# Linear attention with a cosine router: transposes and state updates set at other places in TensorE's and VectorE's order

## The chip, the cores and the metric

The kernel runs on one core of a Trainium2 chip. A core has five engines, each of which works through its own list of instructions in order: TensorE (PE: matmuls and transposes), VectorE (DVE), ScalarE (ACT), GpSimd (POOL) and SyncE (SP, which issues most of the transfers). They wait for each other through semaphores. The metric is the time of one execution on the device, in microseconds (us); several runs are taken and their median is given.

## The reference

Two blocks, one behind the other. The first is a linear attention with a decaying state, for 4 batches, 8 heads, 768 steps and 48 columns a head; the second sends every row of its output to one of 8 experts by a cosine similarity.

```python
for t in range(S):                                    # S = 768, per batch and head
    cur = np.einsum('bhd,bhe->bhde', u[None] * kt, vt)
    y[:, :, t] = np.einsum('bhd,bhde->bhe', rt, state + cur)
    state = w[None, :, :, None] * state + np.einsum('bhd,bhe->bhde', kt, vt)
x = y.transpose(0, 2, 1, 3).reshape(3072, 384)
...
logits = xn @ en.T / tau                              # normed rows, 8 experts
expert_idx = np.argmax(logits, axis=1)
out[mask] = gate_w[mask, None] * (np.maximum(x[mask] @ w1[e], 0) @ w2[e])
```

All numbers are float32.

## The kernel before

**Attention in turns.** The 768 steps are cut into 6 chunks of 128, and a chunk again into two halves of 64. A turn `t` does one chunk of two of the four batches, so there are 12 turns (`TURNS`); `c, bp = divmod(t, 2)` are its chunk and its pair of batches, and `u` (0 or 1) is the batch within the pair. The heads are worked on in 4 pairs.

What a turn does on each engine:

- GpSimd scales the loaded R and K by powers of the decay (`scale_r`, `scale_k`, L377 and L373), half a turn to a turn ahead.
- TensorE transposes R and K of each batch, four 128x128 blocks each (`turn_in`, L393, into banks D0 and D1 for the first batch, D2 and D3 for the second). ScalarE copies them to SBUF (`take_in`: R at L409, K at L407), and VectorE makes a second R, times u (`own_r`, L420).
- TensorE computes the scores (`scores`, L433, 32 small matmuls a batch, into the same D banks). VectorE masks them and puts in the diagonal's own terms (`mask` L448, `own_terms` L455).
- TensorE adds up outer products of K and V (`outer`, L469, 64 small matmuls, into bank U0 for the chunk's first half and U1 for the second). VectorE adds U0 to the state (`half_state`, L485), then U1 to that (`next_state`, L490), and GpSimd applies the decay (`decay_state`, L496).
- In the next turn's time, TensorE makes the outputs: masked scores times V (`with_v`, L524, in two phases of 32), with the state times R between them (`with_state`, L543: 32 matmuls with the state at the chunk's start, `s` = 0, which chunk 0 has not, and 32 with the half state, `s` = 1). `between` (ScalarE, L512) reads one column of each output bank, so that the second phase starts after the first has drained.
- ScalarE copies the outputs to SBUF (`take_y`, L550), TensorE transposes them to rows (`turn_y`, L558, four blocks a batch, into U0 for the first batch and U1 for the second: the banks of the outer products), ScalarE copies the rows (`take_x`, L562), SyncE writes them to DRAM (`keep_x`, L587), and ScalarE takes the sum of squares (`squares`, L593).
- Once in two turns the router's work of a chunk is put in between: `logits` (L600), `turn_logits` (L622), `ranks` (L684 to L687), `put` (L867), and small steps on VectorE; `choose_a` (GpSimd, L639 and L640) works on the sums of squares.

The small matmuls use the array in tiles: 48 or 64 rows by 48 or 64 columns, four at a time. The transposes and `put` use all of it (128 by 128), `logits` strips of 32 columns.

**What sets the order.** Nothing is reordered by a scheduler. `attention` gives each step a time in a plan (`plan.at(time, function, ...)`); the plan is sorted by time and written out, and each engine runs what it has in that order. The times are no clock: they only say what comes before what. A turn is `PERIOD` = 9.4 units long; `at` is its start, `before` and `nxt` the starts of the turns on either side, and `end` that of the last one. So TensorE's order in the middle turns is: scores of both batches, `turn_logits` or `ranks`, `with_v` phase 0, `with_state` (both), `put`, `turn_in` of R and K of the first batch of the next turn, `with_v` phase 1, `outer` of both batches, `turn_in` of R and K of the second batch, `turn_y` of both batches, `logits`. VectorE's order in the second half of a turn is `half_state`, `next_state`, `own_r` of the second batch.

Loads of R, K and V are issued by SyncE some three turns ahead, each once TensorE has reached the instruction that was the last written out before it (`k.last`).

**The experts.** After attention the rows are gathered by expert with indirect transfers, and each expert's two layers follow (L1165 for the first two, then L1243 and L1364/L1383, where products of sums take the place of some matmuls). This part takes the time from some 131 us on.

Of the kernel before, what the change touches and what calls it, by code (L numbers as in the profile page):

```python
# [70 lines left out]
def halves(s):  # L71
    return slice(s * HC, (s + 1) * HC)
# [272 lines left out]
def of(ring, t):  # L345
    return ring[t % len(ring)]
# [111 lines left out]
    )  # L458


def outer(k, t):
    Kw, V = of(k.Kw, t), of(k.V, t)
    last = t // 2 == NCH - 1
    for u in range(2):
        for p in range(NP):
            for s in range(1 if last else 2):
                for par in range(2):
                    h, col = 2 * p + par, (u * NP + p) * D
                    k.last = k.nc.tensor.matmul(  # L469
                        k.U[s][par * DP : (par + 1) * DP, col : col + D],  # L470
                        Kw[halves(s), u, h, :], V[halves(s), u, h, 0:D],
                        start=True, stop=True, skip_group_check=True,
                    )
# [407 lines left out]
def attention(k):  # L881

    plan = Plan()
    P = PERIOD
    end = (TURNS - 1) * P
    for t in range(TURNS):
        at = t * P
        c, bp = divmod(t, 2)
        before, nxt = at - P, at + P
        for i in range(6 if t else 0):  # L890
            when = at - 3 * P + 0.5 + 1.55 * i
            if t < 4:

                if t < 3 and i > 3:
                    continue
                plan.at(when, load, k, t, i // 2 if t > 2 else i % 2, i % 2 if t > 2 else i // 2, slice(0, H), False)
                if t < 3 and i == 3:
                    for v in ((0,), (1, 2))[t - 1]:
                        for w in range(2):
                            plan.at(when + 0.1 * v + 0.01, load, k, v, 2, w, slice(0, H), False)  # L900
                continue
            for j in range(2):
                plan.at(when + 0.75 * j, load, k, t, i // 2, i % 2, slice(j * NP, (j + 1) * NP))
        for u in range(2):
            for which in range(2):

                place = which if t else 1 - which
                if t:
                    plan.at(before + 1.0 + 2 * u + place, scale_k if which else scale_r, k, t, u)
                plan.at(before + 3.3 + 2.35 * u + 0.47 * place, turn_in, k, t, u, which)  # L910
                plan.at(before + 3.8 + 2.4 * u + 0.6 * place, take_in, k, t, u, which)
            plan.at(before + (4.0 if t else 4.75) + 2.6 * u, own_r, k, t, u)
            plan.at(at + 0.9 * u, scores, k, t, u)
            for par in range(2):
                plan.at(at + 0.9 + 1.5 * u + 0.36 * par, mask, k, t, u, par)
                plan.at(at + 1.65 + 1.5 * u + 0.4 * par, own_terms, k, t, u, par)
        if t < TURNS - 1:
            plan.at(at + 4.75, outer, k, t)
            plan.at(at + 5.6, half_state, k, t)
        else:  # L920
            plan.at(at + 5.0, outer, k, t)
            plan.at(at + 5.3, half_state, k, t)
        if c < NCH - 1:
            plan.at(at + 6.2, next_state, k, t)
            plan.at(at + 6.8, decay_state, k, t)
        if t < TURNS - 2:
            a = (1.8, 2.3, 3.3, 4.25, 5.0, 6.65, 7.4, 8.4)
            plan.at(nxt + a[0], with_v, k, t, 0)
            plan.at(nxt + a[1], with_state, k, t)
            plan.at(nxt + a[2], between, k, t)  # L930
            plan.at(nxt + a[3], with_v, k, t, 1)
            for par in range(2):
                plan.at(nxt + a[4] + 0.6 * par, take_y, k, t, par)
            for u in range(2):
                plan.at(nxt + a[5] + 0.45 * u, turn_y, k, t, u)
                plan.at(nxt + a[6] + 0.5 * u, take_x, k, t, u)
                plan.at(nxt + a[6] + 0.1 + 0.5 * u, keep_x, k, t, u)
                plan.at(nxt + a[7] + 0.7 * u, squares, k, t, u)
        else:

            for when, fn, *args in (
                (
                    (3.0, with_v, 0), (3.5, with_state), (4.6, between), (5.6, with_v, 1),
                    (5.65, take_y, 0), (5.7, take_y, 1), (7.6, turn_y, 0), (7.75, take_x, 0), (7.9, turn_y, 1),
                    (7.76, keep_x, 0), (8.5, take_x, 1), (8.51, keep_x, 1), (9.5, squares, 0), (9.55, squares, 1),
                ),
                (
                    (6.8, with_v, 0), (6.82, with_state, (0,)), (7.5, with_state, (1,)), (7.7, between),
                    (7.8, with_v, 1), (8.2, take_y, 0), (8.4, take_y, 1), (10.0, turn_y, 0), (10.02, turn_y, 1),
                    (10.4, take_x, 0), (10.41, keep_x, 0), (10.5, take_x, 1), (10.51, keep_x, 1),  # L950
                    (10.7, squares, 0), (10.75, squares, 1),
                ),
            )[t - TURNS + 2]:
                plan.at(end + when, fn, k, t, *args)
        if bp == 1 and c < NCH - 1:
            plan.at(nxt + 7.6, logits, k, c)
            plan.at(nxt + 8.6, take_logits, k, c)
            then = nxt + P
            plan.at(then + 1.78, turn_logits, k, c)
            if c < NCH - 2:  # L960
                plan.at(then + 2.42, keep_logits, k, c)
                plan.at(then + 6.9, choose_a, k, c)
                plan.at(then + 7.5, choose, k, c)
                plan.at(then + 8.9, scale, k, c)
                plan.at(then + 9.0, exps, k, c)
                then += P
                plan.at(then + 1.79, ranks, k, c)
                plan.at(then + 2.42, placed, k, c)
                plan.at(then + 7.5, places, k, c)
                plan.at(then + 8.7, gate, k, c)  # L970
                plan.at(then + 8.8, values, k, c)
                plan.at(then + 8.9, rows_of, k, c)
                plan.at(then + P + 3.25, put, k, c)
                plan.at(then + P + 3.95, collect, k, c)
            if c == SETTLE[0]:
                plan.at(then + 2.43, count, k, c)
                plan.at(then + 5.0, settle, k, c)
                plan.at(then + 5.05, settled, k)

    c = NCH - 2  # L980
    for t, fn, *args in (
        (1.0, choose_a, k, c),
        (3.96, first_lists, k, 0),
        (4.0, keep_logits, k, c),
        (4.2, choose, k, c),
        (5.5, scale, k, c),
        (6.3, exps, k, c),
        (6.85, ranks, k, c),
        (6.9, placed, k, c),
        (6.95, count, k, c),  # L990
        (7.3, places, k, c),
        (7.4, settle, k, c),
        (7.45, sort_embeddings, k),
        (7.5, sort_counts, k),
        (8.4, gate, k, c),
        (8.8, values, k, c),
        (8.9, rows_of, k, c),
        (11.2, put, k, c),
        (11.25, collect, k, c),
        (11.3, first_lists, k, 1),  # L1000
        (11.35, settled, k),
    ):
        plan.at(end + t, fn, *args)
# [3 lines left out]
    c = NCH - 1  # L1007
# [790 lines left out]
def kernel(  # L1798
# [43 lines left out]
    with tc.manual_schedule(), ExitStack() as long_ctx:  # L1842
        n.long = long_ctx.enter_context(tc.tile_pool(name="long", bufs=1))
        with ExitStack() as attention_ctx:
            n.aconst = attention_ctx.enter_context(tc.tile_pool(name="aconst", bufs=1))
            rings(n)
            build_first(n)
            n.rt = attention_ctx.enter_context(tc.tile_pool(name="rt", bufs=2))
            attention(n)
        with ExitStack() as experts_ctx:  # L1850
            n.gp1 = experts_ctx.enter_context(tc.tile_pool(name="gp1", bufs=1))
            n.gp = experts_ctx.enter_context(tc.tile_pool(name="gp", bufs=4))
            experts(n)
# [29 lines left out]
```

## Time and profile before

| | us |
|---|---|
| median of 3 runs | 421.48 |
| lowest and highest | 415.93, 426.96 |
| the profiled execution | 415.55 |
| its span, first to last instruction | 413.70 |

Its granted TensorE clock was 0.964 of full speed over the span. By engine and stretch of the span (busy us; clock; GB/s moved by the transfers):

| stretch, us | length | PE | DVE | ACT | POOL | clock | GB/s |
|---|---|---|---|---|---|---|---|
| 20 to 35 | 15.0 | 13.21 | 10.38 | 9.96 | 9.75 | 1.00 | 175 |
| 44.4 to 55.3 | 10.9 | 9.81 | 7.32 | 6.55 | 6.58 | 1.00 | 168 |
| 76.1 to 85.3 | 9.2 | 9.20 | 8.10 | 4.48 | 5.21 | 1.00 | 163 |
| 95.7 to 105.7 | 10.0 | 9.49 | 8.06 | 4.08 | 5.13 | 1.00 | 145 |
| 122 to 132 | 10.0 | 8.43 | 5.35 | 2.83 | 1.73 | 0.66 | 150 |
| 152 to 163 | 11.0 | 7.65 | 1.46 | 1.82 | 7.09 | 0.79 | 130 |
| 211 to 414 | 203.0 | 187.84 | 98.61 | 51.65 | 89.11 | 0.97 | 101 |

A profile shows each instruction with its engine, its line in the kernel (L393 is line 393) and its names as output<-input; `x8` is a count of instructions. The matmuls of TensorE overlap in the pipeline, so the busy time of a group is the union of its instructions, and what one more of them costs is seen in the distance of starts. The chain of waits follows the end of the run back, step by step, to what released each instruction or to the one before it on its engine; time that belongs to no instruction that the profile shows stands there as "issue".

### The profile page before, as it was taken

What the parts mean: (1) busy time and instruction counts of PE and PEld (TensorE: products, weight loads), DVE (VectorE), ACT (ScalarE), POOL (GpSimd) and SP (SyncE); (2) the same over time, 40 slices, a digit from 0 to 9 for tenths busy, and PEclk for the clock granted to TensorE, in tenths of its full rate; (3) what the DMA queues carried; (4) which work ended last, traced back from release to release, by engine and by line L of the source; (5) the groups of instructions that cost most, each with busy time, mean ns of one, the idle gap of its engine ahead of it and who ended that gap; (6) DMA issues with size and microseconds to landing.
All of it is one profiled execution on the core that took longest, in us unless ns stands there. A gap on an engine that the chain in (4) does not pass through costs nothing.

```text
span 413.7 us, 12753 instructions
## 1 busy us (share of the span) xinstructions
PE 383.0 (93%) x5055; PEld 349.9 (85%) x5055; DVE 236.4 (57%) x603; ACT 138.2 (33%) x357; POOL 189.2 (46%) x222
## 2 busy tenths in 40 slices
PE   8889899999989996999989997699999999999993
PEld 5778788888878895989779997699999989989982
DVE  7957787878885650532843744155546546465331
ACT  4464546465524521221023212221321321422410
POOL 3875656555530354420377427501753855702002
PEclk9999999999996996899999999689999999999998
DMA  9988788788154573263953553144454446101001
GB/s 157 198 165 174 158 172 181 146 183 179 44 178 142 162 238 104 73 164 93 315 178 90 126 182 93 42 111 136 132 137 142 144 133 199 62 10 57 0 2 65
DMA packets 100232, 54.44 MB, mean 132 GB/s; under 512 B 80897, under 2 KB 95275, under 8 KB 100162
## 3 DMA queue, kind: packets, MB, share of 16 engines
q1 hardware_dynamic: 93218, 43.68, 41.6%
q0 software_dynamic: 4448, 9.45, 7.5%
q8 instruction: 42, 0.69, 0.7%
q10 hardware_dynamic: 2496, 0.40, 0.5%
q14 instruction: 28, 0.23, 0.2%
HBM read 44.25 MB, written 9.58 MB: 130 GB/s over the span
## 4 chain that ended last, share of the span: by engine, by line
PE 76%; issue 9%; DVE 2%; another core or an unknown queue 2%; POOL 1%; ACT 1%; POOLq 0%; DVEq 0%; ACTq 0%
PE ps L1243 9%; PE ps L1383 8%; PE ps L1165 7%; PE ps L1364 6%; PE pu L1243 5%; PE ps L433 4%; PE ps L393 4%; PE pu L1383 4%; PE py L1243 4%; PE py L1383 3%; PE pu L558 3%; PE py L524 3%; PE py L1165 3%; PE py L543 2%; PE pu L469 2%
## 5 line engine op out<-in xcount | busy, mean ns | idle before, releaser
L1123 POOL DMA_INDIRECT G<-xs,quarters x76 | 83.7, 1101 | 50.5 <-issue 38.8
L1342 POOL DMA_INDIRECT out_dram<-y,goes x27 | 28.3, 1048 | 97.0 <-DVE y L1352 41.3
L1165 PE MATMUL ps<-RT,w 128*128 128x128 f32 x204 | 30.1, 299 | 4.4 <-ACT R L1168 1.9
L1165 PEld LDWEIGHTS ps<-RT,w 128*128 128x128 f32 x204 | 27.3, 210 | 5.9 <-issue 2.3
L377 POOL TENSOR_TENSOR Rw<-R,rpow 128x384 f32<-128x384 f32 x22 | 22.8, 1037 | 14.2 <-PE ps L433 8.0
L1243 PE MATMUL ps<-xTe,w 128*128 128x192 f32 (+3 forms) x132 | 27.0, 339 | 0.0
L433 PE MATMUL ps<-RT,KT 48*64 48x128 f32 x768 | 25.3, 275 | 0.2
L433 PEld LDWEIGHTS ps<-RT,KT 48*64 48x64 f32 x768 | 21.1, 132 | 3.7 <-issue 2.5
L373 POOL TENSOR_TENSOR Kw<-K,kpow 128x384 f32<-128x384 f32 x22 | 23.8, 1081 | 0.5 <-DMA R<-in_r_dram 0.5
L1243 PEld LDWEIGHTS ps<-xTe,w 128*128 128x128 f32 x132 | 23.4, 194 | 0.1
L496 POOL TENSOR_TENSOR T<-T,wC 128x384 f32<-128x384 f32 x10 | 8.3, 827 | 27.1 <-DVE T L490 27.1
L448 DVE TENSOR_TENSOR AT<-ps,smask 128x256 f32<-128x256 f32 x48 | 18.6, 414 | 1.2 <-PE ps L433 1.2
L409 ACT COPY RT<-ps 128x512 f32<-128x512 f32 x22 | 12.9, 585 | 18.3 <-PE ps L393 16.9
L455 DVE COPY_PREDICATED AT<-dmask,ps 128x256 f32<-128x256 int32 x48 | 18.5, 441 | 0.0
L1270 ACT ACTIVATE RT<-RT 128x384 f32<-128x384 f32 (+1 forms) x18 | 9.5, 532 | 26.1 <-DVE RT L1182 18.6
L1243 PE MATMUL ps<-Tx,S 128*128 128x192 f32 (+3 forms) x76 | 16.5, 348 | 1.2 <-issue 1.1
L420 DVE TENSOR_TENSOR RT<-ps,uw 128x512 f32<-128x512 f32 x22 | 15.2, 690 | 4.2 <-ACT RT L409 3.9
L393 PE MATMUL ps<-ident,Rw 128*128 128x128 f32 x96 | 15.4, 283 | 2.2 <-DVE AT L455 1.0
L1383 PE MATMUL ps<-T,RT 128*128 128x192 f32 x96 | 17.3, 327 | 0.0
L1270 ACT ACTIVATE hT<-hT 128x432 f32<-128x432 f32 (+2 forms) x18 | 9.7, 541 | 21.2 <-DVE hT L1182 16.1
L1383 PEld LDWEIGHTS ps<-T,RT 128*128 128x128 f32 x96 | 15.9, 190 | 0.9
L469 PE MATMUL pu<-V,Kw 64*64 64x48 f32 x704 | 14.4, 218 | 2.4 <-issue 2.3
(380 smaller groups left out, 917.0 us busy)
## 6 DMA issues: line engine op xcount, KB each, us to landing
w<-in_moe_w_dram SPq DMA_DIRECT2D x96, 128.0 KB
w<-in_moe_w_dram SPq DMA_DIRECT2D x24, 384.0 KB
xs<-X SPq DMA_DIRECT2D x24, 192.0 KB
K<-in_k_dram SPq DMA_DIRECT2D x32, 96.0 KB
R<-in_r_dram SPq DMA_DIRECT2D x32, 96.0 KB
V<-in_v_dram SPq DMA_DIRECT2D x32, 96.0 KB
w<-in_moe_w_dram SPq DMA_DIRECT2D x16, 192.0 KB
V<-in_v_dram SPq DMA_DIRECT2D x8, 192.0 KB
```

What stands on the lines that cost most here:

```text
L373: q.tensor_mul(of(k.Kw, t)[:, u, :, 0:D], of(k.K, t)[:, u] if t else raw(k, 0)[:, u, :, 0:D], k.kpow)
L377: ins = k.nc.gpsimd.tensor_mul(of(k.Rw, t)[:, u, :, 0:D], of(k.R, t)[:, u], k.rpow)
L393: k.last = k.nc.tensor.transpose(bank[:, p * C : (p + 1) * C], pair(src[:, u], p), k.ident)
L433: ins = k.nc.tensor.matmul(k.D[2 * u + par][halves(s), p * C : (p + 1) * C], KT[rows, u, p, halves(s)], RT[rows, u, p, s].rearrange("q j i ...
L469: k.last = k.nc.tensor.matmul(k.U[s][par * DP : (par + 1) * DP, col : col + D], Kw[halves(s), u, h, :], V[halves(s), u, h, 0:D], start=Tru ...
L1123: k.nc.gpsimd.indirect_dma_start(out=k.GG[e % 2][:, g * QUARTER : (g + 1) * QUARTER], out_offset=None, in_=k.xs.rearrange("n (q c) -> (n q ...
L1165: k.last = k.nc.tensor.matmul(ps, w1[:, m, f * 128 : (f + 1) * 128], x_of(k, e, m)[:, cols], start=(m == 0), stop=(m == NK - 1))
L1243: k.last = nc.tensor.matmul(ps[:, i * h : (i + 1) * h], a[:, g, i * 128 : (i + 1) * 128], b, start=start and i == 0, stop=True, skip_group ...
L1270: nc.scalar.activation(out(i, c), out(i, c), ACT.Relu)
L1342: k.nc.gpsimd.indirect_dma_start(out=out[:, :], out_offset=IndirectOffsetOnAxis(ap=k.goes[0:n, e, t : t + 1], axis=0), in_=y[0:n, :], in_o ...
L1364: k.last = k.nc.tensor.matmul(k.two[e][m], a, b, start=(f == 0), stop=(f == NF - 1))
L1383: k.last = nc.tensor.matmul(ps, a(q), b[:, q], start=start and q == 0, stop=True, skip_group_check=True,)
```

## The change

It moves steps in the plan and splits two of them; no matmul, transfer or vector operation is added or taken away.

- `turn_in` and `take_in`, from the second turn on: R and K of a batch get times further apart (2.75 and 3.8, 5.3 and 6.35, where they were 3.3 and 3.77, 5.65 and 6.12).
- `with_state` is called once for each half of the chunk, at 2.3 and 3.3, so R of the first batch comes between the halves and K behind them. `between` moves from 3.3 to 3.75.
- `outer` is called once for each batch, at 4.75 and 5.75, so R of the second batch comes between and K behind.
- `turn_y`, `take_x`, `keep_x` and `squares` of the second batch go 2.8 to 2.55 units later, into the next turn: its `turn_y` stands between the scores of the two batches.
- On VectorE `half_state` goes from 5.6 to 6.16 and `own_r` of the second batch from 6.6 to 6.17: the order becomes `half_state`, `own_r`, `next_state`.
- `choose_a` of the last chunk but one goes from 1.0 to 2.3, behind the squares that it reads.

```diff
-def outer(k, t):
+def outer(k, t, us=(0, 1)):
     Kw, V = of(k.Kw, t), of(k.V, t)
     last = t // 2 == NCH - 1
-    for u in range(2):
+    for u in us:
...
-                plan.at(before + 3.3 + 2.35 * u + 0.47 * place, turn_in, k, t, u, which)
-                plan.at(before + 3.8 + 2.4 * u + 0.6 * place, take_in, k, t, u, which)
-            plan.at(before + (4.0 if t else 4.75) + 2.6 * u, own_r, k, t, u)
+                if t:
+                    plan.at(before + ((2.75, 3.8), (5.3, 6.35))[u][place], turn_in, k, t, u, which)
+                    plan.at(before + ((3.4, 4.4), (6.1, 6.8))[u][place], take_in, k, t, u, which)
+                else:
+                    plan.at(before + 3.3 + 2.35 * u + 0.47 * place, turn_in, k, t, u, which)
+                    plan.at(before + 3.8 + 2.4 * u + 0.6 * place, take_in, k, t, u, which)
+            plan.at(before + ((4.0, 6.17) if t else (4.75, 7.35))[u], own_r, k, t, u)
...
         if t < TURNS - 1:
-            plan.at(at + 4.75, outer, k, t)
-            plan.at(at + 5.6, half_state, k, t)
+            for u in range(2):
+                plan.at(at + 4.75 + u, outer, k, t, (u,))
+            plan.at(at + 6.16, half_state, k, t)
...
-            a = (1.8, 2.3, 3.3, 4.25, 5.0, 6.65, 7.4, 8.4)
+            a = (1.8, 2.3, 3.75, 4.25, 5.0, 6.65, 7.4, 8.4)
             plan.at(nxt + a[0], with_v, k, t, 0)
-            plan.at(nxt + a[1], with_state, k, t)
+            for s in range(2):
+                plan.at(nxt + a[1] + s, with_state, k, t, (s,))
...
             for u in range(2):
-                plan.at(nxt + a[5] + 0.45 * u, turn_y, k, t, u)
-                plan.at(nxt + a[6] + 0.5 * u, take_x, k, t, u)
-                plan.at(nxt + a[6] + 0.1 + 0.5 * u, keep_x, k, t, u)
-                plan.at(nxt + a[7] + 0.7 * u, squares, k, t, u)
+                over = u * (P + 0.5 - a[5])
+                plan.at(nxt + a[5] + over, turn_y, k, t, u)
+                plan.at(nxt + a[6] + over, take_x, k, t, u)
+                plan.at(nxt + a[6] + 0.1 + over, keep_x, k, t, u)
+                plan.at(nxt + a[7] + over, squares, k, t, u)
...
-        (1.0, choose_a, k, c),
+        (2.3, choose_a, k, c),
```

## The prediction

> **What bounds the kernel now.** I read the page first. TensorE is the busiest engine by far, and the chain of work that ended last is mostly its own.
>
> ```profile
> PE 383.0 (93%) x5055; PEld 349.9 (85%) x5055; DVE 236.4 (57%) x603; ACT 138.2 (33%) x357; POOL 189.2 (46%) x222
> ...
> q8 instruction: 42, 0.69, 0.7%
> ...
> PE 76%; issue 9%; DVE 2%; another core or an unknown queue 2%; POOL 1%; ACT 1%; POOLq 0%; DVEq 0%; ACTq 0%
> ```
>
> The change touches attention alone, so the second view is the chain of waits from 0 to 220 us in order of time (columns: start us, us, what). Two turns of it:
>
> ```profile
> 40.50 0.92 PE pu L469 x64
> 41.42 0.59 PE ps L393 x4
> 42.01 1.00 issue
> 43.01 0.60 PE ps L393 x4
> 43.61 0.87 PE pu L558 x8
> 44.48 1.91 PE ps L433 x64
> ...
> 79.01 0.90 PE py L543 x64
> 79.90 1.03 PE pu L867 x8
> 80.94 0.88 PE ps L393 x8
> 81.82 0.62 PE py L524 x32
> 82.44 0.92 PE pu L469 x64
> 83.36 1.02 PE ps L393 x8
> 84.39 0.94 PE pu L558 x8
> 85.32 1.91 PE ps L433 x64
> ```
>
> From 34 to 131 us the chain never leaves TensorE, except for "issue". Every other engine is ahead of it, so in attention a microsecond of TensorE is a microsecond of time. A turn takes 9.1 to 11.4 us (the scores, L433, start at 44.48, 55.35, 64.78, 76.22, 85.32).
>
> Two things in these lines carry the forecast. **First, crossing between transposes and dense stages costs time.** Eight transposes take 0.88 us behind the eight full-array matmuls of L867, but 1.02 to 1.03 us behind small-tile matmuls: 0.14 to enter. The 32 matmuls of L524 behind transposes take 0.62 us, where 32 of L469 (half of 0.92) or L543 (half of 0.90) behind other small ones take 0.46: 0.16 to leave. A detour from a dense stage into transposes and back thus costs **0.30 us, however many transposes it holds**. The individual matmul starts say the same: dense groups of four start 0.058 apart and transposes 0.109, but at the two borders the steps are 0.149, 0.165, 0.202 and 0.107.
>
> **Second, the "issue" gaps.** Counted in recorded matmuls, TensorE stopped for 0.4 us or more at numbers 347, 979, 1232, 1738, 1864, 2370 and 2749. All differences are multiples of about 126 matmuls, 253 instructions with their weight loads. Queue q8 moved 42 packets of 16 KiB. So these gaps look like waits for the next block of instructions: 0.74, 1.00, 1.08, 0.40, 0.95, 0.43 and 0.51, together **5.1 us**. In such a gap TensorE's packet had started 2.3 to 2.5 us before work resumed. From one block's first instruction to the next block's arrival it took 3.8 to 4.6 us; the blocks that stalled held only 3.1 to 3.9 us of work.
>
> **What the Trainium skill says.** "TensorEngine Tiling (Array Packing)", Key Properties: changing the tiling mode, not just the tile, drains TensorE. The trace agrees and prices it: 0.30 us there and back. "Runtime: NRT & Kernel Launch", Instruction fetch mechanics: each engine streams its instructions in 16 KiB blocks of 256, fetching the next while it executes the current one, and the cost of a crossing is mostly hidden. The block size agrees; "mostly hidden" does not hold here, with seven gaps up to 1.08 us.
>
> **The change part by part.** The planner sorts by time and each engine runs in that order, so it can be followed by hand.
>
> *Three splits on TensorE.* No matmul is added. In each turn, though, (a) the first batch's K transposes are parted from its R transposes by the second half of L543; (b) the second batch's are parted by the second batch's half of L469; (c) the second batch's output transposes (L558) leave the block behind K and go between the two score stages of the next turn. Each makes one detour more. (a) has a dense stage between in turns 1 to 10, (b) in 0 to 10, (c) for ten outputs: 31 detours x 0.30 = **+9.3 us**. Bounds: 0.25 each (7.8), if some of the exit overlaps, and 0.35 (10.9). No cover hides this, since TensorE is the chain.
>
> *Instruction waits.* The same instructions run slower, so blocks last longer. A block is 126 of a turn's some 290 matmuls, 44%, and so gets about 0.44 of the turn's extra 1.2 us, 0.5 us. Capped at each gap, the seven shrink to 0.2, 0.5, 0.6, 0, 0.45, 0 and 0: **-3.4 us**. Bounds: -5.1 (all gone) and -1.5 (the fetch gets later as well). Spreading the slow transposes evens the demand for instructions, which favours the larger gain; the fetch competes with loads that are paced by TensorE, which tells nothing.
>
> *The half state and the output transposes.* L485 reads bank pu0 after the outer products; L558's first batch then overwrites pu0. Now:
>
> ```profile
> 83.40 0.56 DVE L485 TENSOR_TENSOR Tmid<-T,pu 128x384 f32<-128x384 f32 x1 [0.67 <-PE pu L469]
> 84.06 0.56 DVE L490 TENSOR_TENSOR T<-Tmid,pu 128x384 f32<-128x384 f32 x1
> 84.22 1.10 PE L558 MATMUL pu<-ident,YT 128*128 128x128 f32 x8
> ```
>
> The last outer matmul started at 83.14, so the read ended 0.82 after it, and eight transposes (R and K) cover that: L558 starts 1.08 after. With the change only K's four lie between; they end their slots 0.64 after it. A release by VectorE reached a transpose 0.15 us later elsewhere (own terms ended 12.25, matmul 12.39), so L558 could start at 0.97: a **new wait of 0.33 us** in ten turns, +3.3 at most. Where an instruction wait lies in the same place it is inside it (about a quarter of the turns): **+2.5**; bounds 0 and 3.6. Behind it on TensorE are L558 and the next scores, so it goes straight into the chain. That the half state is placed ahead of R times u (L420, 0.69 us) keeps the wait from being 0.69 longer; R times u then ends about 1.5 after the last outer matmul, ahead of the second scores that need it, at about 3. Next state follows at 2.1, before the second output transposes (2.5). Those no longer wait for it at all, which they did by 0.07 in four turns (0.94 against 0.87 in the chain): -0.3.
>
> *The rest, at nothing.* ScalarE (33% busy) copies the second output rows and squares them about 3 us later, still before its next evacuations; `between` has 0.73 us of K transposes to hide behind, and ended 0.49 after L543's last start. GpSimd's scaling starts after the first scores and is ready 1 us before its transposes. SyncE's row writes follow the copy; the loads queued behind them wait for the second scores at that point anyway. `choose_a` of the last but one chunk goes 1.3 later because its squares do; GpSimd's next work there (first gather, 5.7 us after the scores' start) begins about 1 us after it would end. If these covers fail, each costs a few tenths a turn; 0 to 2 in all.
>
> Sum: 9.3 - 3.4 + 2.5 - 0.3 = **+8.1 us**. What follows attention starts from TensorE's order too (gathers, paced weight loads), so it moves along. The profiled execution took 415.55 us, span 413.7: 423.6 on that scale. The runs shown lie between 415.93 and 426.96, and their median, 421.48, is 5.9 above the profiled one; I add to the median: **429.5 us**.
>
> **Rivals.** *Wash (some 425):* all gaps vanish and the new wait hides: 9.3 - 5.1 - 0.3 = +3.9. For it: blocks are only 0.4 to 1.1 us too short. Against it: the gaps of 1.0 us lie in blocks that gain less than that. *Worse (some 434):* gaps hardly shrink, 9.3 - 1.5 + 3.3 = +11 to +13. For it: some crossings already took 4.4 to 5.1 us. *Faster:* TensorE also stops at about 122 to 124 us with its block's packet starting only at 122.0, and then runs at half clock to 131 (transposes 0.213 apart against 0.109), and again from 158 to 169 behind waits for weights. If the shift kept the clock up there, it would give back 3.4 and some 5 us, and with all gaps gone and the wait hidden: 3.9 - 2 - 8.4 = -6.5, about 415. It decides only if the stop at 122 shrinks below what lets the clock fall; nothing in the change touches the instructions of that block, so I give it little. *Not doing what it says:* emission is a plain sort, so the order does change; only chunk 0 lacks the first state half, counted above.
>
> **Chances and range.** Likeliest case +8: 0.48 (423 to 436, with the spread of single runs, +-5). Wash 0.27, worse 0.18, faster 0.07. Range 420.5 to 437.5. A difference under 2% (8.4 us, 413 to 430) is about what a measurement of this kernel can't tell from none. The likeliest case lies at that border: slower by over 2% 0.46, within 0.49, faster 0.05.
>
> **What would show it.** In the changed profile's chain: L393 and L558 in fours, each with its dense neighbours at 0.62-like prices; scores parted by four L558; a TensorE wait "L558 <- DVE Tmid L485" of about 0.3, some ten times; fewer and shorter "issue" pieces; turns of 10 to 11 us, attention ending about 8 us later. I am wrong if a four-transpose detour costs under 0.15 us, if turns get shorter, or if the time after attention changes by more than attention does.

## The result and the profile after

The changed kernel is slower: a median of 432.65 us (430.55 to 440.61, five runs) against 420.1 us for the kernel before (412.85 to 426.96, five runs, taken side by side), a ratio of **1.041, 95% interval 1.028 to 1.054**. (Some runs of most kernels here are over 1.5% above the fastest of the same kernel; ratios leave these out on both sides, medians don't.) Its profiled execution had a span of 430.8 us.

The page of the changed kernel, the same lines as of before (busy time and share by engine; the chain that ended last, by engine):

```profile
PE 390.6 (91%) x5055; PEld 348.7 (81%) x5055; DVE 240.8 (56%) x603; ACT 142.2 (33%) x357; POOL 187.3 (43%) x222
```

The lines' shares read alike, but the chain tells another story:

```profile
PE 65%; issue 14%; DVE 9%; POOL 5%; DMA 4%; ACT 1%; another core or an unknown queue 1%; POOLq 0%; SPq 0%; ACTq 0%
```

VectorE has gone from 2% to 9% of it and GpSimd from 1% to 5%. Both come from attention. This is one turn there, the longer pieces of the chain of waits of the changed kernel (start us, us, what):

```profile
93.58 0.56 DVE T L490
94.20 0.83 POOL T L496
95.03 0.99 POOL ssq L639
96.58 0.88 DVE l L665
97.46 0.67 DVE AT L448 x2
98.63 0.63 PE ps L393 x4
99.26 0.59 PE py L543 x32
99.85 0.59 PE ps L393 x4
100.44 0.62 PE py L524 x32
101.52 0.59 PE ps L393 x4
102.11 0.62 PE pu L469 x32
```

Before, this stretch was TensorE alone. Now it runs in a circle through three engines: next state (L490), decay on GpSimd (L496), the router's power on GpSimd (L639), the router's scaling on VectorE (L665), masks (L448), the first R transposes (L393), and on through the turn to the next state. The view of what TensorE waited for, over the whole changed kernel (us in total, times, longest):

```profile
PE ps L393 <- DVE AT L455: 6.7, 8, 1.2
...
PE ps L393 <- POOL Rw L377: 1.1, 2, 0.7
...
PE pu L469 <- issue: 0.5, 2, 0.4
PE pu L558 <- DVE Tmid L485: 0.5, 3, 0.2
```

The transposes of R wait for the own terms: a wait that the kernel before had once, in its first turn. The gaps at the borders of instruction blocks are nearly gone, and the output transposes do wait for the half state, but little.

To compare kernels I use one length: the **ten turns** from the first scores (L433) of the second turn to those of the last, and TensorE's idle time in it, added up from the trace by what ended it. Before: 100.2 us, idle 6.3, of which 5.3 "issue". After: 111.4 us, idle 9.5: own terms 6.4, half state 1.2, GpSimd's scaled R 1.1, "issue" 0.5. So the ten turns grew by 11.2 us, where the medians lie 12.5 apart and the two profiled spans 17.1. Of the rest of the 17.1, 0.7 us lies ahead of the ten turns, 0.5 between them and the first expert layer, and 4.7 behind that: the experts took 281.4 us before and 286.1 after. Over all profiles here they took 276.5 to 281.4 us in the kernel before and those made from it, and 275.5 to 291.8 in those made from the change. Single profiles don't tell whether an edit has a part in that, so I read nothing from it.

One thing in these lengths is not the order of the steps. In the changed kernel's profile the granted clock was 0.5 from 51.5 to 54.9 us. Without its idle time that turn took 12.07 us, where the same turn of experiment 9, at full clock, took 10.61. So about **1.5 us of the 11.2** are the half clock. Neither profile of the kernel before has such a stretch in its ten turns, nor have experiments 1, 2, 3, 5, 7, 9 and 10; experiments 4, 6, 8 and 11 have, with 20.5, 6.8, 13.6 and 6.8 us at half the clock, and half of that is a fair estimate of what it cost them.

### The profile page after: what moved, and what is told of

The parts are those of the page before. It is cut to its first block, busy times and chain, and to the rows that moved or that the text cites. A ratio compares the mean times of both kernels' runs of the same rounds, so it can differ in the third digit from the quotient of the medians.

```text
span 430.8 us, 12728 instructions
## 1 busy us (share of the span) xinstructions
PE 390.6 (91%) x5055; PEld 348.7 (81%) x5055; DVE 240.8 (56%) x603; ACT 142.2 (33%) x357; POOL 187.3 (43%) x222
## 4 chain that ended last, share of the span: by engine, by line
PE 65%; issue 14%; DVE 9%; POOL 5%; DMA 4%; ACT 1%; another core or an unknown queue 1%; POOLq 0%; SPq 0%; ACTq 0%
PE ps L1252 9%; PE ps L1392 7%; PE ps L1373 6%; PE ps L1174 5%; PE pu L1252 5%; PE ps L393 5%; PE pu L1392 4%; PE py L1252 3%; PE py L1392 3%; PE pu L469 3%; PE py L1174 2%; PE py L524 2%; PE py L543 2%; PE pu L1373 2%; PE py L1373 1%
## 5 line engine op out<-in xcount | busy, mean ns | idle before, releaser
L1132 POOL DMA_INDIRECT G<-xs,quarters x76 | 82.4, 1084 | 49.6 <-issue 39.3
L1174 PE MATMUL ps<-RT,w 128*128 128x128 f32 x204 | 29.0, 291 | 3.9 <-ACT R L1177 2.5
L1174 PEld LDWEIGHTS ps<-RT,w 128*128 128x128 f32 x204 | 26.1, 203 | 5.2 <-ACT R L1177 2.9
L496 POOL TENSOR_TENSOR T<-T,wC 128x384 f32<-128x384 f32 x10 | 8.3, 827 | 43.8 <-DVE T L490 29.9
L433 PE MATMUL ps<-RT,KT 48*64 48x128 f32 x768 | 26.8, 277 | 0.1
L433 PEld LDWEIGHTS ps<-RT,KT 48*64 48x64 f32 x768 | 20.8, 132 | 4.7 <-issue 3.5
L1252 PE MATMUL ps<-Tx,S 128*128 128x192 f32 (+3 forms) x76 | 17.8, 369 | 6.1 <-ACT hT L1279 3.3
L373 POOL TENSOR_TENSOR Kw<-K,kpow 128x384 f32<-128x384 f32 x22 | 22.9, 1040 | 0.7 <-DVE Kw L373 0.7
L393 PE MATMUL ps<-ident,Rw 128*128 128x128 f32 x96 | 15.6, 286 | 7.8 <-DVE AT L455 6.7
L1191 DVE TENSOR_TENSOR hT<-ps,kept 128x400 f32<-128x400 f32 (+2 forms) x10 | 5.8, 579 | 27.1 <-PE ps L1252 17.8
L1252 PEld LDWEIGHTS ps<-Tx,S 128*128 128x128 f32 x76 | 14.3, 206 | 8.1 <-ACT hT L1279 3.7
L409 ACT COPY RT<-ps 128x512 f32<-128x512 f32 x22 | 12.9, 586 | 20.5 <-PE ps L393 20.5
L448 DVE TENSOR_TENSOR AT<-ps,smask 128x256 f32<-128x256 f32 x48 | 18.5, 413 | 0.8 <-PE ps L433 0.8
L393 PEld LDWEIGHTS ps<-ident,Rw 128*128 128x128 f32 x96 | 10.2, 141 | 9.8 <-POOL Rw L377 4.9
L524 PE MATMUL py<-AT,V 64*64 64x64 f32 x704 | 16.6, 228 | 1.0 <-issue 1.0
```

Of the source, the lines that this page charges most:

```text
L373: q.tensor_mul(of(k.Kw, t)[:, u, :, 0:D], of(k.K, t)[:, u] if t else raw(k, 0)[:, u, :, 0:D], k.kpow)
L393: k.last = k.nc.tensor.transpose(bank[:, p * C : (p + 1) * C], pair(src[:, u], p), k.ident)
L433: ins = k.nc.tensor.matmul(k.D[2 * u + par][halves(s), p * C : (p + 1) * C], KT[rows, u, p, halves(s)], RT[rows, u, p, s].rearrange("q j i ...
L524: k.last = k.nc.tensor.matmul(y_out(k, t, par, p, u, s), V[halves(s), u, 2 * p + par, :], AT[halves(s), u, par, p * HC : (p + 1) * HC], st ...
L1132: k.nc.gpsimd.indirect_dma_start(out=k.GG[e % 2][:, g * QUARTER : (g + 1) * QUARTER], out_offset=None, in_=k.xs.rearrange("n (q c) -> (n q ...
L1174: k.last = k.nc.tensor.matmul(ps, w1[:, m, f * 128 : (f + 1) * 128], x_of(k, e, m)[:, cols], start=(m == 0), stop=(m == NK - 1))
```

## The experiments

Three theories at the start: the **detours** between tilings of the array alone; the detours and a **closed loop** through VectorE's masks; and the supply of **instructions**. First each of the three splits was undone by itself, and VectorE's router steps were moved.

**1. R of the first batch put back**, with its copy and `between`.

```diff
-plan.at(before + ((2.75, 3.8), (5.3, 6.35))[u][place], turn_in, ...)
+plan.at(before + ((3.3, 3.77), (5.3, 6.35))[u][place], turn_in, ...)
...
-    plan.at(nxt + a[1] + s, with_state, k, t, (s,))
+    plan.at(nxt + a[1] + 0.5 * s, with_state, k, t, (s,))
```

> The changed kernel, with the first batch's R transposes put back behind both state halves, next to its K transposes. Measured: the ten turns from the first scores of the second turn to those of the last (100.2 us in the profile before, 111.4 in the changed one), and TensorE's waits there. Theory 'detours and VectorE's late masks': ten detours fewer, -3.0, and the wait of R's transposes for the own terms (6.4 us in seven turns) goes almost whole, as R comes half a state stage and more later: 102 to 103.5 us. Theory 'detours alone cost': -3.0, so 108.4, with the wait moved on to some other step. Theory 'instructions': the gaps at block borders come back by 1 to 2 us, 104 to 105.

Ten turns 102.96 us; own terms 1.6 us, half state 1.4, "issue" 0.5. Ratio to the kernel before 1.004 (0.998 to 1.011). One split of three undone takes back 8.5 of the 11.2 us, or some 7 of 9.7 without the half clock: nearly three times what its ten detours are worth. The first mask comes as late after the turn's scores as in the change (3.6 to 4.4 us in seven turns); only R's transposes come later. So the position ahead of the second state half, not the detour, is what costs. "Detours alone" is out.

**2. The outer products whole again**, with the old order on VectorE (half state, next state, R times u).

```diff
-plan.at(before + ((4.0, 6.17) if t else (4.75, 7.35))[u], own_r, k, t, u)
+plan.at(before + ((4.0, 6.6) if t else (4.75, 7.35))[u], own_r, k, t, u)
...
-    plan.at(at + 4.75 + u, outer, k, t, (u,))
-plan.at(at + 6.16, half_state, k, t)
+    plan.at(at + 4.75 + 0.1 * u, outer, k, t, (u,))
+plan.at(at + 5.6, half_state, k, t)
```

> The changed kernel, with both batches' outer products in one stage again, the second batch's R and K transposes together behind them, and VectorE's half state, next state and R times u in the old order. Ten turns as defined for the first run, 111.4 us in the changed kernel. Theory 'detours and VectorE's late masks': ten detours fewer, -3.0, and the waits of the output transposes for the half state (1.2 us) go, but VectorE's next state ends earlier by 0.7 us so the masks' wait shrinks too, by up to 3: 105 to 107.5. Theory 'detours alone': 108.4. Theory 'the waits alone cost': 110.2.

Ten turns 101.9 us, ratio 1.006 (1.001 to 1.010). I had expected 105 to 107.5. The own terms cost 1.2 us instead of 6.4 though R's transposes still stand at the early place. The first mask comes 3.0 to 3.9 us after the scores in these turns, up to 0.9 sooner than in the change, where I had counted 0.7. "Issue" is back at 2.4 us.

**3. The output transposes back.**

```diff
-over = u * (P + 0.5 - a[5])
-plan.at(nxt + a[5] + over, turn_y, k, t, u)
+plan.at(nxt + a[5] + 0.45 * u, turn_y, k, t, u)
...
```

> The changed kernel, with the second batch's output transposes, copies, writes and squares back behind the first batch's. Ten turns as defined for the first run, 111.4 us in the changed kernel. Theory 'detours and VectorE's late masks': nine detours fewer, -2.7, but R's transposes then come 0.75 us sooner while the masks, held by VectorE's router steps, do not, so the wait for own terms grows by up to 0.75 in each of the seven turns that wait: 109.5 to 112, with that wait at 9 to 11 us. Theory 'detours alone cost': 108.7, the wait unchanged at 6.4.

Ten turns 109.97 us; own terms 4.7 us, and a new wait of the second output transposes for the next state, 2.8 us in nine turns. Ratio 1.045 (1.035 to 1.056). So taking nine detours away gave next to nothing: inside a loop that something else sets, TensorE's own work is nearly free. The wait did not grow to 9 us as I thought; part of it moved to the next state.

**4. The router's steps behind the masks.** `scale`, `exps`, `gate`, `values` and `rows_of` go behind the masks, `put` and `collect` into the second half of the turn.

```diff
-plan.at(then + 8.9, scale, k, c)
+plan.at(then + P + 4.6, scale, k, c)
...
-plan.at(then + P + 3.25, put, k, c)
+plan.at(then + P + (3.25 if c == SETTLE[0] else 6.34), put, k, c)
```

> The changed kernel, with the router's scaling, gates, values and one-hot rows (scale, exps, gate, values, rows_of) of the first chunks set behind the masks of the turn on VectorE, ahead of the half state, and put and collect behind them. Nothing is left out. Ten turns as defined for the first run, 111.4 us in the changed kernel. Theory 'detours and VectorE's late masks': the wait of R's transposes for own terms falls from 6.4 to under 1 us, the detours stay: 104.5 to 106. Theory 'the wait is only where TensorE would stand anyway, for instructions': the wait goes but gaps for instructions take its place, 109 to 111.

Ten turns 117.8 us, ratio 1.028 (1.017 to 1.039). The wait for own terms is gone, as the loop theory says, but `put` (L867) at its new place waits 5.1 us in three turns for the next state, which reads the same bank, and two stretches of 3.4 us and one of 13.7 ran at half the clock, worth some 10 us. With the new wait and the clock in it, this run settles nothing about the sum.

**5. The next state ahead of R times u**, everything else as in the change.

```diff
-plan.at(before + ((4.0, 6.17) if t else (4.75, 7.35))[u], own_r, k, t, u)
+plan.at(before + ((4.0, 6.6) if t else (4.75, 7.35))[u], own_r, k, t, u)
```

> The changed kernel, with VectorE's next state ahead of the second batch's R times u, as it was before the change. Ten turns from the first scores of the second turn to those of the last: 111.4 us in the changed kernel, 6.4 of it waits of R's transposes for own terms. Theory 'a closed loop of outer products, states, decay, router steps, masks and R's transposes sets the turn': the next state ends 0.7 us sooner, GpSimd's decay and the power behind it too, so the loop is shorter by up to 0.7 in the turns in which VectorE waits for that power (some half of them): 106.5 to 109. Theory 'R times u behind the state is late for the scores': a new wait of the second scores, 111.4 or more. Theory 'no part in it': 111.4 within 0.7.

Ten turns 108.98 us, own terms 3.1 us (6.4): the loop does go through the next state. In time little came of it: 0.9 us without the half clock of the change, with "issue" back at 2.6 us. The ratio, 1.016 (0.996 to 1.035), is too wide to add to that.

**6. The power ahead of the decay on GpSimd.**

```diff
-plan.at(then + 6.9, choose_a, k, c)
+plan.at(then + 6.7, choose_a, k, c)
```

> The changed kernel, with GpSimd's power of the squares (choose_a) ahead of the decay of the state in the turns that have both. Ten turns: 111.4 us in the changed kernel. Theory 'closed loop': where VectorE waits for the power (four turns), its masks come up to 0.8 to 1 us sooner, and the decay later by 1.3, which is still ahead of its use: 108 to 109.5. Theory 'VectorE's own work in the turn sets the masks': 111 to 111.8.

Ten turns 114.2 us; four runs of 422.72 to 432.47 us against 411.31 to 419.16 of the kernel before, from which no ratio was taken. Two stretches of 3.4 us at half the clock are in it, one more than in the change, so some 1 us of the 2.8 that it is longer is the edit's. It is no faster, and the loop as I had drawn it doesn't explain that: the power came in time in all four turns, yet from the end of the next state to the first mask it took 0.5 us less than in the change in two of them and 1.4 us more in the other two. The timeline shows why. Two engines in it, first the change (start us, us, engine, line, operation, output<-input):

```profile
94.20 0.83 POOL L496 TENSOR_TENSOR T<-T,wC 128x384 f32<-128x384 f32 x1 [6.00 <-DVE T L490]
94.25 0.82 DVE L650 TENSOR_TENSOR l<-lg,mx 128x32 f32<-128x32 f32 x1
...
94.98 1.04 POOL L639 TENSOR_TENSOR ssq<-ssq,half 128x4 f32<-128x4 f32 x1
95.11 0.19 DVE L652 SCALAR_TENSOR_TENSOR er<-l,rev 128x32 f32<-128x32 f32 x1
```

then this kernel, in the same turn, one of the two that got longer:

```profile
90.97 0.83 POOL L496 TENSOR_TENSOR T<-T,wC 128x384 f32<-128x384 f32 x1 [4.76 <-DVE T L490]
91.02 0.83 DVE L650 TENSOR_TENSOR l<-lg,mx 128x32 f32<-128x32 f32 x1
...
91.78 1.00 POOL L377 TENSOR_TENSOR Rw<-R,rpow 128x384 f32<-128x384 f32 x1
91.88 0.94 DVE L652 SCALAR_TENSOR_TENSOR er<-l,rev 128x32 f32<-128x32 f32 x1
...
92.73 1.00 POOL L373 TENSOR_TENSOR Kw<-K,kpow 128x384 f32<-128x384 f32 x1
92.86 0.19 DVE L654 TENSOR_REDUCE back<-er 128x4 f32<-128x32 f32 x1
93.08 0.72 DVE L655 TENSOR_TENSOR cum_oh<-er,back 128x32 f32<-128x32 f32 x1
```

and the kernel before, where R times u (L420) stood between the next state and L650, and the decay was almost over when L650 began:

```profile
84.60 0.69 DVE L420 TENSOR_TENSOR RT<-ps,uw 128x512 f32<-128x512 f32 x1
84.69 0.83 POOL L496 TENSOR_TENSOR T<-T,wC 128x384 f32<-128x384 f32 x1 [2.71 <-DVE T L490]
...
85.42 0.19 DVE L650 TENSOR_TENSOR l<-lg,mx 128x32 f32<-128x32 f32 x1
85.47 1.04 POOL L639 TENSOR_TENSOR ssq<-ssq,half 128x4 f32<-128x4 f32 x1
85.65 0.19 DVE L652 SCALAR_TENSOR_TENSOR er<-l,rev 128x32 f32<-128x32 f32 x1
```

A subtraction of 128x32 numbers that takes 0.19 us alone takes 0.83 beside the decay, and ends with it; in experiment 6 L652, L655 and L658 end with the scalings. The reduction L654 (one input) keeps its 0.19 us in the middle of a scaling. "SBUF — State Buffer" of the Trainium skill, Who interferes with whom, says that a VectorE instruction with two inputs in SBUF contends with a GpSimd instruction that reads SBUF, and that `tensor_reduce` does not; the trace agrees with both for the decay and the scalings, and gives the price: up to the whole GpSimd operation. It does not agree for the power: L639 reads SBUF too, 128x4 numbers, and beside its 1.04 us L652 kept 0.19 us. That is why two turns of experiment 6 got longer: with the power gone from between the decay and the scalings, the scalings came onto these steps. The masks and R times u, whose one large input lies in PSUM, kept 0.41 and 0.69 us in the change and before.

Added up over the ten turns, VectorE's router steps took 18.3 us before and 24.1 us in the change (L650 0.82 for 0.19, L834 0.60 for 0.16, L858 1.1 to 1.2 for 0.42); 29.1 here, 20.5 in experiment 5, and 18.3 again in experiment 2. That is about what experiment 2 did better than I had expected. So the theory was recast: with R times u ahead of the next state, the decay falls onto VectorE's router steps, and these hold up the masks.

**7. One split alone on the kernel before**: the output transposes between the scores.

> The kernel before, with one part of the change alone: the second batch's output transposes go between the two score stages of the next turn. Ten turns: 100.2 us before, of which 5.2 are gaps at borders of instruction blocks. Theory 'a detour costs 0.30 us': nine more in the ten turns, +2.7, and 1 to 2.5 us of the gaps go: 100.5 to 102. Theory 'detours cost nothing, the waits made the change slow': 98 to 100 (gaps shrink, nothing added).

Ten turns 101.55 us, "issue" 4.1; own terms none, router steps 18.3 us. Without idle time that is 96.0 us against 93.9 before: **0.24 us for each of nine detours**. Ratio 1.016 (1.000 to 1.033).

**8. The other way round**: all small-tile stages of a middle turn together.

```diff
...
-plan.at(at + 4.75, outer, k, t)
-plan.at(at + 5.6, half_state, k, t)
+plan.at(at + (3.3 if 0 < t < TURNS - 2 else 4.75), outer, k, t)
+plan.at(at + (4.3 if 0 < t < TURNS - 2 else 5.6), half_state, k, t)
...
```

> The kernel before, turned the other way: in the middle turns all small-tile stages stand together (scores, with_v, with_state, outer, with_v), and all sixteen transposes of R and K stand behind them, next to the output transposes; the states follow the outer products at once. Eight or nine detours fewer. Ten turns: 100.2 us before. Theory 'detours alone': 97.5. Theory 'instruction blocks arrive one in 3.6 to 4 us': 256 small matmuls in a row use two blocks in some 5 us, so the gaps grow from 5.2 to 12 us or more and eat the gain: 102 to 105.

Ten turns 111.2 us; four runs of 421.62 to 435.07 us against 411.31 to 419.16, again without a ratio. "Issue" grew to 6.6 us, less than I had said; another 5 us went to waits of `ranks` and `outer` for VectorE's router steps and their readers, and 13.6 us of this run's ten turns stood at half the clock, worth some 6 us. The trace counts six detours fewer, not eight or nine. In the seven turns at full clock, with four of the six, TensorE's work without idle time was 62.3 us, against 64.1 in the mean of the two profiles of before. So fewer detours did save work here; the idle time (13.4 us against 6.3) and the clock took more than that back.

**9. The decay later: the recast theory's test.** GpSimd's decay moves behind the next turn's scalings, away from VectorE's router steps. Nothing on TensorE or VectorE changes place.

```diff
-plan.at(at + 6.8, decay_state, k, t)
+plan.at(at + P + 4.5, decay_state, k, t)
```

> The changed kernel, with GpSimd's decay of the state one turn's length later: behind the next turn's four scalings, still ahead of its use. Ten turns: 111.4 us in the changed kernel, where VectorE's router steps behind the next state took 24.1 us (18.3 before): L650 0.82 (0.19), L834 0.60 (0.16), L858 1.2 (0.42), each ending with a GpSimd operation. Theory 'GpSimd's operations hold up VectorE's small ones, and these the masks': L650 and L834 fall to 0.2, the wait for the power goes, and R's transposes wait for own terms 1.5 to 4 us in place of 6.4 (L858 may still meet the scalings): 106 to 109. Theory 'R times u ahead of the next state is what lengthens the loop': L650 and L834 fall but the masks come as late, 110.5 or more.

Ten turns **104.5 us**, a little below the range that I had given; own terms 0.4 us. TensorE's idle time fell from 9.5 to 3.8 us; the other 1.2 us of the 6.9 are about what the half clock had cost the change. Ratio 1.016 (1.007 to 1.024), where the change has 1.041. The turn of the chain above, in the timeline of this kernel:

```profile
88.59 0.55 DVE L490 TENSOR_TENSOR T<-Tmid,pu 128x384 f32<-128x384 f32 x1
...
89.27 0.19 DVE L650 TENSOR_TENSOR l<-lg,mx 128x32 f32<-128x32 f32 x1
...
90.03 1.00 POOL L377 TENSOR_TENSOR Rw<-R,rpow 128x384 f32<-128x384 f32 x1 [3.79 <-PE ps L433]
90.20 0.93 DVE L658 TENSOR_TENSOR_SCAN counts<-on,cum_oh 128x40 f32<-128x40 f32 x1
...
93.20 0.63 PE L393 MATMUL ps<-ident,Rw 128*128 128x128 f32 x4
...
93.89 0.82 POOL L496 TENSOR_TENSOR T<-T,wC 128x384 f32<-128x384 f32 x1
```

From the end of the next state to the first R transpose it is 4.1 us here and 4.5 us in the chain of the change, and TensorE arrives without waiting (no idle time is noted on its row). The decay starts 0.7 us behind that, where VectorE masks out of PSUM.

In this turn, though, VectorE gained nothing by L650: it took 0.19 us for 0.82, but L658 now meets a scaling and takes 0.93 for 0.24. What the turn gained is VectorE's wait for the power, which on GpSimd no longer stands behind the decay: 0.33 us here and in one more turn, 1.05 in each of two others. In the three turns without a power there is no such wait, and the held-up steps alone are seen. The change first, then this kernel:

```profile
81.85 0.83 POOL L496 TENSOR_TENSOR T<-T,wC 128x384 f32<-128x384 f32 x1 [4.15 <-DVE over L828]
...
82.09 0.60 DVE L834 SCALAR_TENSOR_TENSOR lo<-hi,rank 128x4 f32<-128x4 f32 x1
...
83.68 1.00 POOL L377 TENSOR_TENSOR Rw<-R,rpow 128x384 f32<-128x384 f32 x1 [1.00 <-PE ps L433]
83.75 1.22 DVE L858 TENSOR_TENSOR QV<-HV,cum_oh 128x256 f32<-128x256 f32 x1
```

```profile
99.26 0.16 DVE L834 SCALAR_TENSOR_TENSOR lo<-hi,rank 128x4 f32<-128x4 f32 x1
...
100.79 0.43 DVE L858 TENSOR_TENSOR QV<-HV,cum_oh 128x256 f32<-128x256 f32 x1
100.83 1.24 POOL L377 TENSOR_TENSOR Rw<-R,rpow 128x384 f32<-128x384 f32 x1 [6.12 <-PE ps L433]
```

From the end of the next state to the first mask these turns took 4.5 to 4.6 us in the change and 3.6 here. L858 now starts ahead of the scaling, keeps its 0.43 us, and the scaling is the one that takes longer. So the late decay lengthened the loop in two ways, by holding up VectorE and by holding up the power on GpSimd; which of the two acted differs by turn. The router steps took 20.4 us in all (24.1; 18.3 before).

**10. Both of experiments 5 and 9.**

> The changed kernel with both: the decay behind the next turn's scalings, and VectorE's next state ahead of the second batch's R times u. Ten turns: 111.4 us in the changed kernel. Theory 'detours plus late masks': the masks' wait is nearly gone (under 1.5 us), the 29 detours stay, at 0.23 to 0.30 each 6.7 to 8.7 over the kernel before, less 4 to 5 us of instruction gaps, plus some 1 us of the output transposes' wait for the half state: 103 to 105.5. Theory 'instructions set the pace anyway': 100 to 102.

Ten turns 107.9 us, own terms 2.0; ratio 1.024 (1.015 to 1.033). I was wrong that the two would add. With R times u behind the next state, VectorE's router steps begin some 0.2 us later against the scores than in experiment 9, and L655 (0.97 us for 0.22) and L658 both meet the scalings. In experiment 9 L655 just passes (0.22). A shift of 0.2 us here decided over most of a microsecond in each of four turns.

**11. The router's lone transposes moved to R's and K's**: eight detours fewer than before.

> The kernel before, with the lone transposes or full-array matmuls of the router (turn_logits and ranks of chunks 0 to 3) moved from between scores and with_v to the first batch's R and K transposes, and their readers on VectorE behind the masks: eight detours fewer. Ten turns: 100.2 us before. Theory 'detours cost 0.23 to 0.30 us, instruction blocks arrive one in 3.6 to 4 us': 1.8 to 2.4 less work, of which the gaps take back half or more: 99 to 100.2. Theory 'detours alone': 97.8 to 98.4.

Ten turns 103.9 us; "issue" 6.7 us (5.3), a wait of 1.5 for scaled R in one turn, and two stretches of 3.4 us at half the granted clock. Ratio 1.019 (1.006 to 1.032). In the eight turns at full clock the work without idle time came to 72.9 us, against 74.2 and 74.4 in the two profiles of before, with seven detours fewer: 0.20 us saved by each. Idle time took back 2.4 us of the ten turns and the clock some 3. "Detours alone" would have given 98.

**12. The kernel before, once more.**

> The kernel before, unchanged, for a second profile: how far the ten turns (100.2 us in the first), the gaps at block borders (5.2) and the time behind attention (some 281 us from the first expert layer's start to the end) come out the same. If the block borders are a matter of instruction count, the gaps lie at the same matmuls again, with other lengths; if they are chance, elsewhere.

Ten turns 99.98 us, "issue" 4.5; ratio to itself 0.999 (0.992 to 1.006). Its "issue" stops of 0.3 us or more are at matmuls 347, 979, 1738, 1864 and 2370, five of the first profile's seven, and at 2623 and 3002, again (to within nine) multiples of 126 behind 347, with other lengths (1.43 us the longest). In other orders of the stages they come at the same numbers too: at 347, 1232 and 1864 in experiment 7, at 348, 979 and 1233 in experiment 8. So they belong to the instruction count and not to the stage that stands there, and the ten turns repeat to 0.2 us.

No version here beats the kernel before. Two that take back one split each (experiments 1 and 2) come within 0.6% of it.

## Why the prediction was right or wrong

The direction was right and the measured time lies in the range, but the likeliest sum was +8.1 us where the medians moved by 12.5, and a term was missing. That it lies in the range is in good part luck. The three larger terms of the forecast measured 6.9 - 4.8 + 1.2 = +3.3 us in the ten turns, close to the rival "wash" (+3.9); experiment 9, where hardly any other term is left, is 4.4 us longer than the mean of the two profiles of before. The wait that the forecast did not have made up the rest.

- **Detours: right in kind, a little dear.** The trace counts 29 more in the ten turns. From experiment 9 (104.5 less 3.8 idle, against 93.8 in the mean of the two profiles of before) they cost 6.9 us, 0.24 each; experiment 7 gives 0.24 again, experiments 1 and 2 give 0.25 and 0.20, 5 and 10 give 0.26, and experiment 11 gives 0.20 for each one less. Experiment 3 stands apart with 0.35; there the output transposes also stop in the middle for the next state. I had 0.30 each, 9.3 in all, from 0.14 to enter and 0.16 to leave in the chain; why less of it remains in most of the sums isn't shown.
- **Instruction waits: right, more was regained.** 5.3 us became 0.5, a gain of 4.8 in the ten turns where I took 3.4.
- **Half state: right in place, half in size.** 1.2 us in eight of the ten turns, 0.15 us or so each, where I had 0.33 and a sum of 2.5. The second output transposes no longer wait, as said.
- **"The rest, at nothing": the step that failed.** I listed ScalarE, GpSimd and SyncE as covers there and allowed 0 to 2 us for all of them, but not the masks that must free R's bank before R's transposes. That wait is the largest single new item, 6.4 us. Moving R ahead of the second state half brought it up to the masks' time (experiment 1). The order half state, R times u, next state, which I counted only as a gain of 0.69 us on one wait, set the masks back: from the fifth turn on the next state ended 0.6 to 2.6 us ahead of the next scores before, and from 0.7 ahead to 0.4 behind them in the change. The stretch from there to the first mask stayed as long (3.3 and 4.0 us) in the turns with the power, which waits behind the decay on GpSimd. In the other turns VectorE's idle time went out of it, but the held-up steps filled it. R times u, gone from that stretch, thus made nothing shorter there. Experiments 1, 2 and 9 each take this wait away by another road, and most of the time with it. With the wait goes the premise "in attention a microsecond of TensorE is a microsecond of time": in experiment 3 nine detours fewer brought nothing.
- With the measured terms, 6.9 - 4.8 + 1.2 + 6.4 + 0.5 (scaled R 1.1, over the 0.6 of both GpSimd waits before; the second profile of before has 1.4 of these, so this term may be chance) - 0.4 (a wait of before for a VectorE step at L298, gone) comes to 9.8 of the 11.2 us. The 1.5 us of the half clock are the rest.
- **Rivals.** "Wash" needed the new waits to hide; they didn't. "Worse" came nearest in time, but by the wrong cause: it said that the gaps would hardly shrink. "Faster" found nothing: the half clock behind attention was there again (136.8 to 143.6).

## What to carry to other kernels

When a step is moved up in a hand-made order, list everything that must have let go of its destination, not only what feeds it: here the bank of the R transposes, held by masks that nothing in the diff mentions. A kernel whose bound engine has no idle time can still be a few tenths of a microsecond from a loop through other engines, and once the loop closes, that engine's own savings can be worth nothing, as in experiment 3. And before an operation of GpSimd is shifted, look at what VectorE does at that moment with two inputs in SBUF.

## What the hardware showed that I had not expected

- A VectorE instruction of 0.19 us stretched to 0.83 us beside GpSimd's 0.83 us decay, and to 0.94 beside a 1.0 us scaling, each ending with it. Beside GpSimd's power of 128x4 numbers (1.04 us) it kept 0.19. Where VectorE's L858 started 0.04 us ahead of a scaling, it kept 0.43 us and the scaling took 1.24; where it started 0.07 us behind one, it took 1.22. Moving one late GpSimd operation a turn took 5.7 us of TensorE's idle time out of ten turns.
- A change of the array's tiling there and back cost 0.20 to 0.26 us net in seven runs that changed their number by 7 to 29, and 0.35 in one.
- TensorE stopped for up to 1.9 us at fixed matmul numbers, multiples of about 126 apart, in both profiles of the kernel before and in other orders of the stages. That its supply of instructions is behind it is my reading of these distances and of the 16 KiB packets on q8.
- In all fourteen profiles the granted clock was either full or half, and every half stretch that ended before the run did lasted 3.4 us or two, three or four times that.
